# Small set-up work of a four-layer state-space kernel computed on VectorE in place of GpSimd, with a new order table

## The chip, the cores and the metric

The kernel runs on one core of a Trainium2 chip. The time is the device time of one execution in microseconds (us). Each kernel was run several times, and kernels that are compared ran on the same chip in the same rounds. All runs told here fell into one state: no run was more than 1.5% above the fastest of its kernel. The engines go by the names of the profile: PE is TensorE, PEld its weight loads, DVE is VectorE, ACT is ScalarE, POOL is GpSimd.

## The reference, cut to what matters

Two kinds of layers alternate, on a sequence of 2048 tokens with 640 channels: a complex diagonal state-space layer (S5) and a long convolution with a gate.

```python
x = x + A(layernorm(x))      # S5: 640 complex states
x = x + B(layernorm(x))      # gate times a long convolution of k*v
x = x + A(layernorm(x))      # the same weights again
x = x + B(layernorm(x))

def A(x):
    dt = exp(log_dt); Lam_bar = exp(dt * Lam)             # 640 complex numbers
    B_bar = ((Lam_bar - 1) / Lam)[:, None] * Bmat         # the S5 factor
    h[t] = Lam_bar * h[t-1] + x[t] @ B_bar.T
    return 2 * real(h @ Cmat.T) + x * Dskip

def B(q):
    k_shift = 4-tap causal convolution of k; kv = k_shift * v
    y = irfft(rfft(kv) * rfft(ssm_k)) + kv * ssm_D        # the same for both layers
    return q * y
```

`y` and the S5 weights depend on no layer's input. The kernel computes them in a set-up of some 165 us and then streams the layers' matmuls.

## The kernel before

A small planner in the kernel's own Python lists every piece of work as a task with an engine (or a choice of two), an estimated cost and what it depends on. It simulates the engines with these costs, takes the free task with the highest rank, and emits the tasks in the order of their simulated starts. The program fixes that order for each engine: a piece that is late holds up what stands behind it in its engine's queue (in the trace of after, an eviction starts at 31.23 us, behind 25 small instructions that take 3.3 us).

```python
t.rank = t.path + t.bias if WHEN is None else 0.001 * t.path - WHEN.get(t.name.partition(":")[0], 0)
...                                                       # cut
order.sort(key=lambda t: (t.start, t.idx))
for t in order:
    t.emit(t.eng)
```

`WHEN` is the order table: one number for a group of tasks ("a_b10" stands for all five tasks "a_b10:0" to "a_b10:4").

The two pieces of GpSimd work that the argument turns on multiply an identity by Lam_bar (15 diagonal matrices of 128 x 128, so that TensorE can scale B by matmuls), and compute the S5 factors in 24 instructions of five elements for each partition (a 25th, the reciprocal, is VectorE's):

```python
def diag(dst, scal, n):
    nc.gpsimd.tensor_tensor(dst, ident[:, None, :].to_broadcast([P, n, P]), scal[:, :, None].to_broadcast([P, n, P]), ALU.mult)

def e_lamd(_):                                            # L401 in the profile
    diag(s_ld.get().rearrange("p i j n -> p (i j) n"), st["lam"][:].rearrange("p i j -> p (i j)"), 15)
t_ld = S.add("a_lamd", "pool", 3.4, [t_lam], e_lamd, uses=[s_ld])

def e_f(_):                                               # L411 to L440
    v = nc.gpsimd
    v.tensor_tensor(den[:], lre, lre, ALU.mult)
    v.tensor_tensor(t2[:], lim, lim, ALU.mult)
    v.tensor_tensor(den[:], den[:], t2[:], ALU.add)
    nc.vector.reciprocal(inv[:], den[:])
    ...                                                   # 21 more of [128, 5], cut
t_f = S.add("a_f", "pool", 5.5, [t_lam], e_f)
```

Beside them stand, in the same stretch, the four-tap convolution of k (TensorE, L1064) with its eviction (a copy out of the matmuls' result memory, which is also the product with v), on VectorE (L1070), evictions of matmuls on ScalarE (L296) or VectorE (L298), and the first piece of a rotation table on VectorE (L552, L553).

## Time and profile before

| | before |
|---|---|
| time, median of 3 runs | 360.56 us (360.41 to 360.77) |
| span of the profiled run | 358.5 us |
| TensorE busy | 324.3 us, 90% |
| VectorE busy | 321.8 us, 90% |
| ScalarE busy | 253.2 us, 71% |
| GpSimd busy | 24.4 us, all of it before 60 us |

Two engines at 90% for the whole span leave little idle time on either for more work. They do not say which of them is the limit at a given time; for that one reads stretches of 10 us, which the prediction shows. One line also belongs here. It is the last 5 us in which TensorE still works (stretch; busy us of PE, PEld, DVE, ACT, POOL with instruction counts; PE clock, DMA share, GB/s):

```profile
345.00:350.00 5.00, 2.83 (x24) 1.64 (x23) 4.90 (x13) 1.99 (x6) 0.00 (x0) 1.00 0.30 121
```

TensorE is busy for 2.83 us after 345 us. The last matmuls in its timeline (start, duration, what) say the same:

```profile
347.10 0.72 PE L773 MATMUL ps<-W,b 128*128 128x128 bf16 x10
347.66 0.22 PE L773 MATMUL ps<-DD,b 128*128 128x128 bf16 x1
```

TensorE ends at 347.88 us and VectorE at 355.3 us.

### The profile page before, as it was taken

To read this page: it belongs to the slowest core of one execution; us is meant where nothing else is said; L and a number is where in the kernel's file an instruction comes from. 1 tells how busy PE (TensorE), PEld (TensorE's weight loads), DVE (VectorE), ACT (ScalarE), POOL (GpSimd) and SP (SyncE) were. 2 spreads that over 40 slices of the span, in tenths; PEclk is the share of its full clock that TensorE was granted. 3 is DMA by queue.
4 is the path that set the end of the run, shared out by engine and by line. 5 is a ranking of instruction groups with operands and counts; after the bars stand their busy time and mean duration, and the time that the engine had idled before them with its cause. 6 is when DMAs were issued, how large, how long until landed. Compare 5 with 4: busy or idle time off the path is not lost.

```text
span 358.5 us, 8291 instructions
## 1 busy us (share of the span) xinstructions
PE 324.3 (90%) x3467; PEld 242.3 (68%) x3493; DVE 321.8 (90%) x482; ACT 253.2 (71%) x399; POOL 24.4 (7%) x57
## 2 busy tenths in 40 slices
PE   2888899978997989999999999999999999999980
PEld 1357867867685978886776686688655788756550
DVE  8979999777899669989997998999999799999996
ACT  6589976989499999784598199796618681106861
POOL 6447200000000000000000000000000000000000
PEclk9999999999999999999999999999999999999996
DMA  9999999989996970966095722450032043000231
GB/s 202 227 169 190 205 193 196 235 156 201 241 249 125 237 159 2 144 121 206 2 206 140 273 76 48 117 129 2 14 61 76 0 112 112 1 2 0 85 136 73
DMA packets 118711, 45.90 MB, mean 128 GB/s; under 512 B 111629, under 2 KB 112914, under 8 KB 118674
## 3 DMA queue, kind: packets, MB, share of 16 engines
q1 hardware_dynamic: 118528, 45.36, 59.1%
q8 instruction: 27, 0.44, 0.5%
q14 instruction: 10, 0.08, 0.1%
q10 hardware_dynamic: 146, 0.01, 0.0%
HBM read 17.38 MB, written 7.86 MB: 70 GB/s over the span
## 4 chain that ended last, share of the span: by engine, by line
PE 62%; ACT 14%; DVE 11%; DMA 5%; issue 4%; POOL 2%; SPq 1%; ACTq 0%; DVEq 0%; POOLq 0%
PE ps L773 31%; PE ps L687 9%; PE ps L684 9%; ACT b L296 8%; PE ps L522 4%; PE ps L1064 4%; DMA b<-b 2%; DVE b L298 2%; ACT b L466 1%; DMA b<-in_A_C_im_dram 1%; DMA b<-in_A_C_re_dram 1%; SPq L462 1%; PE ps L1214 1%; DVE b L1070 1%; PE ps L1215 1%
## 5 line engine op out<-in xcount | busy, mean ns | idle before, releaser
L296 ACT ACTIVATE b<-ps 128x1024 bf16<-128x1024 f32 (+3 forms) x121 | 105.9, 957 | 28.9 <-PE ps L687 22.2
L773 PEld LDWEIGHTS <-b 128*128 128x128 bf16 x880 | 67.6, 98 | 48.2
L773 PE MATMUL ps<-W,b 128*128 128x512 bf16 (+1 forms) x632 | 95.4, 299 | 0.4
L684 PE MATMUL ps<-b,BT 128*128 128x256 bf16 x400 | 56.7, 273 | 2.4 <-ACT b L296 1.7
L687 PE MATMUL ps<-b,BT 128*128 128x256 bf16 x400 | 56.8, 273 | 0.0
L722 DVE TENSOR_TENSOR_SCAN b<-rtab,b 128x1290 bf16<-128x1290 f32 x16 | 44.6, 2832 | 0.2
L684 PEld LDWEIGHTS <-BT 128*128 128x128 bf16 x400 | 38.7, 98 | 7.2 <-issue 1.8
L687 PEld LDWEIGHTS <-BT 128*128 128x128 bf16 x400 | 39.1, 98 | 4.5
L595 ACT ACTIVATE junk<-b,nmean 128x640 bf16<-128x640 f32 x48 | 39.8, 828 | 1.5
L640 ACT ACTIVATE b<-b,nmr,rstd 128x640 bf16<-128x640 f32 (+1 forms) x42 | 35.7, 916 | 2.8 <-DVE nmr L607 2.0
L1133 PE MATMUL ps<-b,b 128*128 128x128 bf16 x170 | 35.1, 219 | 2.4 <-ACT b L296 1.4
L1136 PE MATMUL ps<-b,b 128*128 128x128 bf16 x170 | 35.3, 219 | 0.0
L1135 PE MATMUL ps<-b,b 128*128 128x128 bf16 x150 | 32.9, 220 | 0.0
L1138 PE MATMUL ps<-b,b 128*128 128x128 bf16 x150 | 32.9, 219 | 0.0
L298 DVE CAST b<-ps 128x1024 bf16<-128x1024 f32 (+2 forms) x28 | 28.0, 1024 | 4.7 <-PE ps L1138 2.3
L781 ACT ACTIVATE b<-ps 128x640 f32<-128x640 f32 x15 | 10.5, 701 | 26.4 <-PE ps L773 26.4
L773 PE MATMUL ps<-G,b 128*128 128x128 bf16 (+1 forms) x151 | 26.5, 295 | 0.5
L1064 PE MATMUL ps<-b,fd 128*128 128x512 bf16 x75 | 20.6, 415 | 2.8 <-ACT b L296 1.9
L470 DVE SCALAR_TENSOR_TENSOR W<-b,s_F 128x640 bf16<-128x640 bf16 x20 | 17.2, 880 | 3.7 <-ACT b L466 3.5
L466 ACT ACTIVATE b<-b,s_F 128x640 f32<-128x640 bf16 x20 | 16.5, 832 | 5.2 <-DMA b<-in_A_C_im_dram 4.0
L590 ACT ACTIVATE nmean<-sums 128x4 f32<-128x4 f32 (+1 forms) x15 | 3.0, 201 | 22.7 <-DVE b L785 19.3
L1214 PE MATMUL ps<-b,b 128*128 128x128 bf16 x160 | 18.4, 220 | 0.5 <-ACT b L296 0.5
(210 smaller groups left out, 571.6 us busy)
## 6 DMA issues: line engine op xcount, KB each, us to landing
b<-in_A_x_dram SPq DMA_DIRECT2D x8, 640.0 KB, 5.9
b<-ysd SPq DMA_DIRECT2D x8, 640.0 KB, 3.9
b<-in_B_ssm_k_dram SPq DMA_DIRECT2D x5, 512.0 KB, 6.4
kvd<-b SPq DMA_DIRECT2D x5, 512.0 KB, 3.8
b<-kvd SPq DMA_DIRECT2D x5, 512.0 KB, 5.1
ysd<-b SPq DMA_DIRECT2D x5, 512.0 KB, 4.6
out_dram<-b SPq DMA_DIRECT2D x8, 320.0 KB, 2.2
W<-in_A_B_im_dram SPq DMA_DIRECT2D x1, 800.0 KB
```

What stands on the lines that cost most here:

```text
L296: nc.scalar.activation(out, in_, ACT.Copy)
L298: nc.vector.tensor_copy(out, in_)
L595: nc.scalar.activation(small.junk, src(q), ACT.Square, bias=st["nmean"][:, i:i + 1], scale=1.0, accum_out=st["ssq"][:, i:i + 1])
L640: nc.scalar.activation(dst, src, ACT.Identity, bias=st["nmr"][:, i:i + 1], scale=st["rstd"][:, i:i + 1])
L684: nc.tensor.matmul(pb[:, jj, c2, :], lhsT=aw["BT1"][:, c2, j, k, :], rhs=uT[:, k, 0:2, :].rearrange("p t i -> p (t i)"), start=(k == 0), s ...
L687: nc.tensor.matmul(pb[:, jj, c2, :], lhsT=aw["BT0"][:, c2, k, j * P:(j + 1) * P], rhs=uT[:, k, 2:4, :].rearrange("p t i -> p (t i)"), star ...
L722: nc.vector.tensor_tensor_scan(gv, rt, gv, 0.0, ALU.mult, ALU.add)
L773: nc.tensor.matmul(pc[:, o0:o1], lhsT=lh, rhs=rh, start=(n == 0), stop=(n == len(ops) - 1))
L1064: nc.tensor.matmul(pk[:, 512 * b:512 * (b + 1)], lhsT=s_ds.get()[:, l, :], rhs=kT[:, t0:t0 + 512], start=(l == 0), stop=(l == 3))
L1133: nc.tensor.matmul(ps[:, g, 0, :], lhsT=T["Cf"].get()[:, q, :], rhs=are, start=True, stop=single)
L1135: nc.tensor.matmul(ps[:, g, 0, :], lhsT=T["Sf"].get()[:, q, :], rhs=A[:, 2 * q + 1, :], start=False, stop=True)
L1136: nc.tensor.matmul(ps[:, g, 1, :], lhsT=T["NSf"].get()[:, q, :], rhs=are, start=True, stop=single)
```

## The change

The intent: take the diagonal matrices of Lam_bar and the S5 factors off GpSimd, where they take 3.39 and 6.8 us and where an instruction of VectorE beside them (L552) takes 1.99 us, against 0.82 in after; cut the rest of GpSimd's work into shorter instructions; write LayerNorm rows contiguously and make one product of four; and give every task its own entry in the order table, with TensorE's slow start in the planner's simulation (it doubles TensorE's estimates before 16 us; in the trace of before, matmuls of 512 columns start 0.427 us apart until 17.6 us and 0.216 us apart after it). An entry of two numbers also says how much longer the task's first engine must be busy before its second may take it.

```diff
 WHEN = {
-    "yt_io0": -1077.9, "yt_ph0": -1019.3, "yt_sin0": 190.5, ...        # cut: one entry per group
+    "kv_mm0:0": 17.79, "kv_ev0:0": 19.87, ... "a_b1e0:0": (32.68, 1.5), ...   # cut: one per task
-            t.rank = t.path + t.bias if WHEN is None else 0.001 * t.path - WHEN.get(t.name.partition(":")[0], 0)
+            t.rank, t.wait = t.path + t.bias, 0.3
+            if WHEN is not None:
+                when = WHEN[t.name]
+                t.rank, t.wait = (-when[0], when[1]) if isinstance(when, tuple) else (-when, 0.3)
+                if eng == "pe" and now < self.COLD:                     # COLD = 16.0
+                    t.est *= 2.0
 # S5 set-up
-        diag(s_ld.get()..., st["lam"]..., 15)
-    t_ld = S.add("a_lamd", "pool", 3.4, [t_lam], e_lamd, uses=[s_ld])
+        diag(nc.vector, s_ld.get()..., st["lam"]..., 15)
+    t_ld = S.add("a_lamd", "dve", c_tt(15 * P), [t_lam], e_lamd, uses=[s_ld])    # 1.12
-        v = nc.gpsimd
-    t_f = S.add("a_f", "pool", 5.5, [t_lam], e_f)
+    t_f = S.add("a_f", "dve", 1.9, [t_lam], e_f)
-        diag(aw["DD"][:], st["pf"][:, 3, :], NJ)
+        for j in range(NJ):
+            diag(nc.gpsimd, aw["DD"][:, j:j + 1], st["pf"][:, 3, j:j + 1], 1)
 # four-tap convolution: the diagonals one at a time
-            nc.gpsimd.tensor_tensor(s_ds.get(), ident..., skf..., ALU.mult)      # [P, 4, P]
+            for l in range(4):
+                nc.gpsimd.tensor_tensor(s_ds.get()[:, l], ident, skf..., ALU.mult)   # [P, P]
 # LayerNorm rows contiguous
-                ln_apply(nc, eng, st, q, s_u.get()[:, :, slot, :], src(q).rearrange("p (k e) -> p k e", e=P))
+                ln_apply(nc, eng, st, q, s_u.get()[:, slot * D:(slot + 1) * D], src(q))
 # gate: one product for four rows
-                    nc.vector.tensor_tensor(b, b, s_Y.get()[:, q, :], ALU.mult)   # for each of 4 rows
+                    nc.vector.tensor_tensor(b, b, s_Y.get(), ALU.mult)            # once, 4 rows
```

Some of the planner's costs were changed too, by up to some 0.3 us. `c_tt(n)` is 0.1 + 0.00053 n, the planner's cost in us of a product of bf16 with bf16.

## The prediction

> **What bounds the kernel now.** I read the page first (busy shares and the slices), then stretches of 10 us, then the chain of waits, and last the timeline of the two places where the chain leaves TensorE: the set-up at 24 to 40 us and the end.
>
> ```profile
> span 358.5 us, 8291 instructions
> PE 324.3 (90%) x3467; PEld 242.3 (68%) x3493; DVE 321.8 (90%) x482; ACT 253.2 (71%) x399; POOL 24.4 (7%) x57
> PE   2888899978997989999999999999999999999980
> ```
>
> Two engines are at 90%, TensorE and VectorE, so neither can be relieved alone. The slices show TensorE short of full only in the first 18 (up to some 160 us) and in the last two. By stretches (busy us of PE, PEld, DVE, ACT, POOL):
>
> ```profile
> 20.00:30.00 10.00, 9.08 (x108) 6.78 (x109) 7.92 (x21) 9.92 (x21) 4.33 (x5) 1.00 0.95 161
> 30.00:40.00 10.00, 8.07 (x154) 6.84 (x152) 9.51 (x11) 9.44 (x15) 7.92 (x27) 1.00 1.21 228
> ...
> 300.00:310.00 10.00, 9.95 (x90) 8.68 (x89) 9.86 (x12) 2.42 (x3) 0.00 (x0) 1.00 0.01 3
> ...
> 340.00:350.00 10.00, 7.83 (x69) 4.85 (x68) 9.53 (x23) 6.36 (x16) 0.00 (x0) 1.00 0.39 136
> 350.00:360.00 10.00, 0.00 (x0) 0.00 (x0) 5.26 (x9) 0.85 (x3) 0.00 (x0) 0.60 0.17 66
> ```
>
> From 165 to 342 us TensorE streams without a break, and VectorE is nearly full beside it while ScalarE has room (2.42 of 10). After 342 us TensorE has no more matmuls, and VectorE works off a queue. The end of the chain of waits says the same (start, duration, what):
>
> ```profile
> 28.33 3.40 POOL b L401
> ...
> 338.08 3.82 PE ps L773 x28
> 341.92 0.83 DVE b L785 x2
> 343.20 0.82 DVE b L822
> ...
> 353.61 0.81 DVE b L805
> 354.44 0.89 DVE b L809
> ```
>
> The span has therefore three parts: some 165 us of set-up and long convolution where TensorE, VectorE and ScalarE take turns as the bound; 177 us of pure TensorE; and an end of 358.5 - 341.9 = 16.6 us, of which VectorE's queue is 355.3 - 341.9 = 13.4 and the last store 3.2. The one long GpSimd piece on the chain is the diagonal matrices of lambda, at 28.33. Its neighbourhood in the timeline:
>
> ```profile
> 28.33 3.39 POOL L401 TENSOR_TENSOR b<-ident_bf,s_lam 128x1920 bf16<-128x1920 bf16 x1 [1.74 <-DVE s_lam L395]
> 32.70 1.33 POOL L413 TENSOR_TENSOR s_den<-s_den,s_t 128x5 f32<-128x5 f32 x1
> ```
>
> ```profile
> 30.42 1.99 DVE L552 TENSOR_SCALAR b<-rtab 128x1290 f32<-128x1290 f32 x1
> 32.44 1.53 DVE L553 SCALAR_TENSOR_TENSOR b<-b,rtab 128x1290 f32<-128x1290 f32 x1
> ```
>
> L552 ends at 32.41, only 0.69 us after GpSimd let go at 31.72; L413, five elements wide, takes 1.33 us and ends at 34.03, just after L553 at 33.97. Each engine held the other up.
>
> [...] about 30.42 to 31.72, 1.3 us, of L552 is a wait. [...] L818 (all bf16, 640 wide) has a mean of 487 ns, L822 (one operand fp32, the same width) 825 ns. [...] the first 16 matmuls 512 wide in the chain take 5.91 us (369 ns each), a later run of 8 takes 1.73 us (216 ns). [...] 640 wide costs 487 ns, 2560 wide (L708) 1494, not 4 x 487 = 1948.
>
> **The change, part by part.**
>
> Lambda diagonals to VectorE. Removed from GpSimd: 3.39 us. Added to VectorE: 1920 elements. The scalars are fp32, so by the L822 rate (or L1070: 1024 in 1.22 us, 1.19 ns an element at most; slope between 640 at 825 and 1024 at 1220 is 1.03 ns) I expect 0.1 + 1.04 x 1920 = 2.1 us, not the 1.1 that the kernel's own table assumes. It takes away the 1.3 us wait of L552, and the matmuls on lambda can start 3.4 - 2.1 = 1.3 us earlier.
>
> S5 factors to VectorE. 24 small instructions that took GpSimd from 31.68 to 38.45, 6.8 us. On VectorE dependent small instructions start 0.21 us apart (24.11, 24.32, 24.52, 24.73 in the angle reduction), independent ones 0.07 to 0.15. With half of each: 12 x 0.21 + 12 x 0.1 = 3.7 us of VectorE. The first scaling of C (L466) started at 37.05, 0.34 us after its factor was ready at 36.71, so this was a real wait; now the factors may be ready 4 us earlier.
>
> Shorter GpSimd instructions (shift diagonals and skip diagonals one matrix at a time): the total stays near 5 x 1.05 + 1.25 = 6.5 us, but no VectorE instruction waits for a whole 1.05 us. At 12.93 one 128x1 instruction of VectorE (L963) took 1.04 us in place of 0.15; I count 1 us saved.
>
> LayerNorm rows written contiguously. The VectorE form with fp32 in is 745 ns over 12 uses; the one use near the end that already writes contiguously took 0.61. At most 12 x 0.15 + 6 x 0.1 = 2.4 us, say 1.5 since ScalarE does the larger part of them.
>
> One product for four rows: 28 x L818 at a start-to-start of 0.45 us (12.6) become 7 of 2560 at 1.45 (10.2): 2.4 us less VectorE, spread over the TensorE-bound part.
>
> VectorE in sum: + 2.1 + 3.7 - 1.3 - 1.0 - 1.5 - 2.4 = -0.4 us. Nothing, in total; but the additions lie before 40 us and the savings after 165, where VectorE's queue sets what is left for the end.
>
> TensorE: the same matmuls, so the same time. With N / 2.4 GHz + 2.8 ns for each (the 256-wide ones start 0.109 us apart) they come to 315 us; the stretch from the first matmul (6.4) to the last (341.9) is 335.5. About 20 us are gaps and cold clock (2.4 us of it in the 16 matmuls above), all before 165 us. Counting the cold clock changes no instruction: it only makes the order fit better there.
>
> The order table. Its entries grow like planned starts; I take no time from them, only the order. It puts all of the last layer's products but one row's ahead of the last matmuls: behind TensorE's end then lie one eviction with residual (0.75), four u and four m (8 x 0.80), two pairs of small statistics (0.7), and perhaps one row of the block before (0.8): 8.7 us, against 13.4. The end would be 4.7 us shorter. But this work is done earlier, in a stretch where VectorE already has 95% or more, so part of it comes back as a later end of TensorE unless evictions go to ScalarE. I give back 2.5 of it. In the first part the shorter wait for lambda and the factors are worth 1.3 on the chain, but VectorE was at 9.5 of 10 there and gets 5.8 us more work, less the 2.3 of waits: I count 0.5 us gained from the better packing. Sum: 4.7 - 2.5 + 0.5 = 2.7, so 360.56 - 2.7 = 357.8 us.
>
> **Rivals.** (a) The fine order closes the early gaps: of the 20 us some 6 could go, and with the shorter end the time would be about 351. For it: one entry for each task frees the four rows and the five groups from one common rank. Against it: in 20 to 60 us VectorE, ScalarE and TensorE all have over 80%, so a gap closed on one is opened on another, and the added VectorE work lies just there. (b) The mis-sized VectorE work (2.1 for 1.1, 3.7 for 1.9 assumed) pushes the whole fixed order back by the 2.8 us that the plan lacks, at a time when VectorE is the bound, and TensorE waits: 360 to 362. For it: queues are in order, so a late piece holds up all behind it. Against it: VectorE had 2 us idle in 20 to 30. (c) [...] its removal gives the full 4 us at which the factors come earlier: about 355. Against it: the table still loads C for the weights later than the factors are ready, so weights are not waiting for them.
>
> **Range and chances.** The middle is 357.8; (a) and (c) pull down, (b) up. 8 times in 10 between 353.5 and 361.2. Faster by over 2% means below 353.35, which needs (a) in the main: 0.11. Slower by over 2% means above 367.8, which nothing here but a badly held-up queue would do: 0.02. Within 2%: 0.87.
>
> **What would show it.** TensorE's busy time unchanged within 2 us, 177 us or a little more of unbroken TensorE at the end, VectorE's busy time within 3 us of 321.8, GpSimd down from 24.4 to about 15, the time from the last matmul to the last VectorE instruction 8 to 10 us in place of 13.4, and the lambda diagonals at about 2.1 us on VectorE. It is wrong if TensorE's last matmul ends before 338 us (early gaps closed), if the end stays at 13 us, or if a wait of TensorE on VectorE of over 2 us shows up in 25 to 45 us.

## The result and the profile after

| | before | after |
|---|---|---|
| time, median of 4 runs | 360.49 us (360.18 to 360.77) | 365.30 us (363.55 to 366.90) |
| ratio after/before | | 1.0133, 95% interval 1.0085 to 1.0180 |
| span of the profiled run | 358.5 | 365.2 |
| TensorE's last matmul ends | 347.88 | 353.95 |
| VectorE's last instruction ends | 355.3 | 361.98 |

A ratio is the mean time of one kernel's fast runs over that of the other's fast runs of the same rounds, so it is not quite the ratio of the medians beside it. The change made the kernel slower by 1.3%, about 4.8 us, outside the range on record. The profiled run of after is the slowest of its four (366.9), so of the 6.7 us between the spans some 1.6 belong to that run.

The page of after: span, busy times, PE's slices and the clock that it was granted (tenths of full speed, 40 slices of 9.1 us).

```profile
span 365.2 us, 8269 instructions
PE 327.1 (90%) x3463; PEld 246.1 (67%) x3493; DVE 319.6 (88%) x488; ACT 251.6 (69%) x397; POOL 22.9 (6%) x51
PE   2597998799987999999999999999999999999970
PEclk9998999999999899999999999999999999999995
```

VectorE has 2.2 us less work than before and TensorE 2.8 us more, for the same matmuls. The two slices of the clock that read 8 can account for these 2.8 us: the granted clock was halved for 3.41 us from 32.6 us and for 3.41 us from 118 us, in which the same matmuls take up to 3.4 us longer in all (those of 128 columns start 0.107 us apart instead of 0.056). The stretches (columns as above):

```profile
20.00:30.00 10.00, 9.03 (x97) 5.96 (x97) 9.59 (x26) 7.52 (x14) 3.69 (x11) 1.00 0.78 174
30.00:40.00 10.00, 7.60 (x115) 7.04 (x112) 7.45 (x20) 6.71 (x10) 0.00 (x0) 0.83 1.25 228
...
110.00:120.00 10.00, 7.43 (x96) 5.98 (x95) 9.76 (x28) 9.07 (x14) 0.00 (x0) 0.90 0.77 156
```

In 20 to 30 us VectorE went from 7.92 to 9.59: the moved work. In the next 10 us all three engines do less than before (TensorE 8.07 to 7.60, at a lower clock too; VectorE 9.51 to 7.45; ScalarE 9.44 to 6.71). When all engines are less busy at once, somebody waits for somebody. VectorE's queue from 24 us (start, duration, what):

```profile
24.76 2.16 DVE L487 TENSOR_TENSOR b<-ident_bf,s_lam 128x1920 bf16<-128x1920 bf16 x1
26.84 1.22 DVE L1169 TENSOR_TENSOR b<-ps,b 128x1024 bf16<-128x1024 f32 x1
27.97 0.30 DVE L496 TENSOR_TENSOR s_den<-s_pf 128x5 f32<-128x5 f32 x1
...
31.16 0.16 DVE L525 TENSOR_SCALAR s_F<-s_g 128x5 f32<-128x5 f32 x1
31.23 1.22 DVE L1169 TENSOR_TENSOR b<-ps,b 128x1024 bf16<-128x1024 f32 x1
32.37 0.82 DVE L638 TENSOR_SCALAR b<-rtab 128x1290 f32<-128x1290 f32 x1
```

The 25 small instructions of the factors (L496 to L525) hold the queue from 27.97 to 31.23, 3.3 us, and the eviction L1169 stands behind them. TensorE needs the buffer that this eviction empties:

```profile
30.06 0.22 PE L588 MATMUL ps<-b,tab 128*128 128x128 bf16 x1
32.51 0.22 PE L1232 MATMUL ps<-b,b 128*128 128x128 bf16 x1 [2.23 <-DVE b L1169]
...
33.03 0.31 PE L1235 MATMUL ps<-b,b 128*128 128x128 bf16 x1
33.14 0.31 PE L1237 MATMUL ps<-b,b 128*128 128x128 bf16 x1
```

The bracket is the reading: TensorE stood idle for 2.23 us and was released by that eviction. After it the matmuls of 128 columns start 0.107 us apart instead of 0.056, for 3.41 us: the granted clock was halved (0.50 in 34 to 36 us).

The end of the chain of waits, and TensorE's last group:

```profile
346.07 3.82 PE ps L859 x28
351.02 2.94 DVE b L924 x4
...
358.58 1.68 DVE b L905 x2
```

```profile
353.23 0.72 PE L859 MATMUL ps<-W,b 128*128 128x128 bf16 x10
```

The chain hands over from TensorE to VectorE at 349.9 us, while TensorE goes on until 353.95. From the last matmul to the last VectorE instruction are 8.0 us here and 355.3 - 347.9 = 7.4 us before. The end did not become shorter. So nearly all of the difference in the spans, 6.1 of 6.7 us, is that TensorE finishes later.

To see when TensorE falls behind, the matmuls that had been done by a given time were added up from the traces, each at its length at full clock by the planner's own cost (n / 2400 + 0.0028 us for n columns, as in the prediction, so 0.056, 0.109 and 0.216 us for 128, 256 and 512 columns, the distances at which such matmuls start in the trace of before; 316.1 us in all for each kernel). This table was worked out so; it is the lead (+) or lag (-) against before, in us of matmul work. Some matmul records are missing from the traces (3467 matmuls for 3493 weight loads before); second counts that treat the gaps otherwise agree with it within about 1.1 us, so only its larger steps should be read.

| by (us) | after | after, work on GpSimd | before, work on VectorE | before, factors alone on VectorE |
|---|---|---|---|---|
| 20 | -0.75 | -1.07 | +0.75 | +0.54 |
| 30 | -0.81 | -0.62 | +0.38 | +0.32 |
| 35 | -2.51 | +0.64 | -0.86 | +0.46 |
| 40 | -2.43 | +1.32 | -1.98 | -1.23 |
| 50 | -1.69 | +1.80 | -2.28 | -1.71 |
| 60 | -3.03 | -0.71 | -2.20 | -1.56 |
| 120 | -5.64 | -2.47 | -2.44 | -2.39 |
| 150 | -6.99 | -2.30 | -2.09 | -2.03 |
| 200 to 340 | -6.1 | -1.4 | -3.1 | -2.5 |

The last three columns are experiments, told next. After about 170 us no column changes any more: the rest is TensorE alone, and whatever is lost before is carried to the end.

### The profile page after: what moved, and what is told of

The parts are those of the page before. It is cut to its first block, busy times and chain, and to the rows that moved or that the text cites. A ratio compares the mean times of both kernels' runs of the same rounds, so it can differ in the third digit from the quotient of the medians.

```text
span 365.2 us, 8269 instructions
## 1 busy us (share of the span) xinstructions
PE 327.1 (90%) x3463; PEld 246.1 (67%) x3493; DVE 319.6 (88%) x488; ACT 251.6 (69%) x397; POOL 22.9 (6%) x51
## 4 chain that ended last, share of the span: by engine, by line
PE 65%; DVE 14%; ACT 8%; DMA 6%; issue 3%; SPq 2%; POOL 0%; DVEq 0%; ACTq 0%; POOLq 0%
PE ps L859 31%; PE ps L770 10%; PE ps L773 10%; ACT b L382 4%; PE ps L1163 2%; PE ps L1208 2%; DMA b<-in_B_v_dram 2%; DMA b<-kvd 2%; DVE bs L706 2%; DMA b<-in_A_x_dram 2%; DVE b L1169 2%; PE ps L1232 1%; PE ps L1235 1%; DMA b<-in_A_C_im_dram 1%; PE ps L1237 1%
## 5 line engine op out<-in xcount | busy, mean ns | idle before, releaser
L382 ACT ACTIVATE b<-ps 128x1024 bf16<-128x1024 f32 (+3 forms) x123 | 109.7, 949 | 33.4 <-PE ps L773 23.9
L859 PE MATMUL ps<-W,b 128*128 128x128 bf16 (+1 forms) x629 | 95.6, 298 | 0.6
L1232 PE MATMUL ps<-b,b 128*128 128x128 bf16 x170 | 35.9, 224 | 5.2 <-DVE b L1169 2.2
L726 ACT ACTIVATE b<-b,nmr,rstd 128x640 bf16<-128x640 f32 (+1 forms) x36 | 30.9, 912 | 8.6 <-DVE nmr L693 7.7
L1235 PE MATMUL ps<-b,b 128*128 128x128 bf16 x170 | 36.4, 225 | 0.0
L1237 PE MATMUL ps<-b,b 128*128 128x128 bf16 x150 | 33.9, 226 | 0.0
L1234 PE MATMUL ps<-b,b 128*128 128x128 bf16 x150 | 33.8, 225 | 0.0
L384 DVE CAST b<-ps 128x1024 bf16<-128x1024 f32 (+2 forms) x26 | 26.4, 1024 | 7.6 <-issue 3.4
L1313 PE MATMUL ps<-b,b 128*128 128x128 bf16 x160 | 19.6, 219 | 3.1 <-ACT b L382 2.5
L1314 PE MATMUL ps<-b,b 128*128 128x128 bf16 x160 | 19.5, 219 | 1.1 <-DVE b L1294 1.1
L1163 PE MATMUL ps<-b,fd 128*128 128x512 bf16 x74 | 19.1, 394 | 1.2 <-DVE b L1169 0.7
L552 ACT ACTIVATE b<-b,s_F 128x640 f32<-128x640 bf16 x20 | 16.8, 841 | 3.2 <-DMA b<-in_A_C_im_dram 2.0
```

The costliest lines, as they stand in the source:

```text
L382: nc.scalar.activation(out, in_, ACT.Copy)
L726: nc.scalar.activation(dst, src, ACT.Identity, bias=st["nmr"][:, i:i + 1], scale=st["rstd"][:, i:i + 1])
L859: nc.tensor.matmul(pc[:, o0:o1], lhsT=lh, rhs=rh, start=(n == 0), stop=(n == len(ops) - 1))
L1163: nc.tensor.matmul(pk[:, 512 * b:512 * (b + 1)], lhsT=s_ds.get()[:, l, :], rhs=kT[:, t0:t0 + 512], start=(l == 0), stop=(l == 3))
L1232: nc.tensor.matmul(ps[:, g, 0, :], lhsT=T["Cf"].get()[:, q, :], rhs=are, start=True, stop=single)
L1234: nc.tensor.matmul(ps[:, g, 0, :], lhsT=T["Sf"].get()[:, q, :], rhs=A[:, 2 * q + 1, :], start=False, stop=True)
```

## The experiments

The theory after reading the two traces was that of the queue (Q): the moved work stands in VectorE's queue between 25 and 40 us, in front of evictions that TensorE needs, and the delay is carried to the end. The rivals: the new order table itself is worse; the half clock that follows a gap of TensorE is what costs; the planner was given wrong costs, and right ones would have led to a good order; and, for the hope behind the change, that it gains something if VectorE no longer waits beside GpSimd's long instructions. Fifteen kernels were run; all gave correct results. The time after "against" is that of the kernel before in the same rounds. It lay between 359.64 and 360.50 us, so the ratio is to be read, rather than the absolute times of the expectations. After itself was timed in four runs only: its 1.0133 is known to about 0.5%, so a difference from after of less than 0.5% (1.7 us) is not clear of the noise.

### First: the move and the order apart

**after, with both pieces of work on GpSimd.** The order is planned as in after; only the engine that computes is put back.

```diff
-        diag(nc.vector, s_ld.get()..., 15)
+        diag(nc.gpsimd, s_ld.get()..., 15)
     def e_f(_):
+        v = nc.gpsimd
```

> The changed kernel with the lambda diagonals and the S5 factors emitted on GpSimd again; the order of every engine's other work stays as in the changed kernel. Theory Q (queue: the 2.16 and 3.3 us now stand in VectorE's queue ahead of a PSUM product that TensorE waits for, the gap at 30 to 32.5 us, and the half clock that follows it): the gap and the half clock at 32.6 to 36 us go, some 4 us, so 361 to 362 us. Rival O (order: the new table itself is worse, whatever engine does these two): 364 to 366, as the changed kernel. Rival G (GpSimd takes 3.4 and 6.8 us for them, TensorE waits for the diagonals): a wait on GpSimd of over 1 us before the lambda matmuls, 363 or more.

Measured: 361.87 us (361.80 to 362.21, 5 runs) against 359.82; ratio 1.0061 [1.0045, 1.0078]. Putting the work back on GpSimd gives back 1.0133 / 1.0061 = 1.0072, 0.7% or 2.6 us (give or take 0.5%). The remaining 0.6% (2.2 us) is there with all the arithmetic on its old engine. Rival G fell: the list of TensorE's waits in 24 to 48 us is empty here.

**before, with both on VectorE.** Again the order stays as it was planned.

```diff
-        diag(s_ld.get()..., 15)
+        nc.vector.tensor_tensor(s_ld.get()..., ident..., st["lam"]..., ALU.mult)
     def e_f(_):
-        v = nc.gpsimd
```

> The kernel before with only these two pieces of work moved to VectorE, order table and all else as before. Theory Q: VectorE is full from 26 to 50 us, so 5.5 us more of work[...] delays its evictions: 362 to 364 us. Rival O: the move itself is harmless, 359.5 to 361.

Measured: 363.57 us (362.66 to 364.81, 5 runs) against 359.82; 1.0108 [1.0082, 1.0134]. In the order for which it was not planned the move costs 1.1%. TensorE's timeline shows two gaps with VectorE's eviction as the releaser (in the brackets):

```profile
31.68 0.22 PE L502 MATMUL ps<-b,W 128*128 128x128 bf16 x1 [2.09 <-DVE b L298]
...
38.21 0.40 PE L1110 MATMUL ps<-FA,b 64*128 64x128 bf16 x8 [1.18 <-DVE b L298]
```

The move is a loss in the old order and in the new one.

**after, with the factors behind the next eviction.** In VectorE's queue the 25 instructions trade places with the eviction that they held up.

```diff
         order.sort(key=lambda t: (t.start, t.idx))
+        move task "a_f" to just behind task "kv_ev1:0"
```

> The changed kernel with one task moved: the S5 factors (24 small VectorE instructions) go behind the next PSUM product of the shift convolution rather than ahead of it. Theory Q: TensorE's gap at 30 to 32.5 us closes and no half clock follows, the time falls by 3 to 4 us to 361 to 362.5. Rival O: the time stays at 364 to 366, because what is won at 35 us is lost again in the waits at 100 to 150 us.

Measured: 363.60 us (362.83 to 363.97, 4 runs) against 359.82; 1.0103 [1.0083, 1.0124]. The gap of 2.23 us and the half clock at 32.6 us are gone (the mean granted clock of the run is 0.979 all the same, as in after); the longest wait of TensorE on VectorE in 24 to 48 us is now this one (waits: us in total, times, longest):

```profile
PE ps L591 <- DVE BT L388: 1.1, 1, 1.1
```

TensorE's lag at 40 us is gone (within the 1.1 us of the count), but at 60 us it lags by 1.0 and at the end by 2.8. Only 0.3% came back, less than the noise of after. So that one gap does not explain the loss: in this trace it was closed and nearly all of the loss stayed. That the 3.3 us of VectorE then make another eviction late (the 1.1 us above) is a reading of the trace.

**after, with the true costs given to the planner.**

```diff
-    t_ld = S.add("a_lamd", "dve", c_tt(15 * P), ...)
+    t_ld = S.add("a_lamd", "dve", 2.1, ...)
-    t_f = S.add("a_f", "dve", 1.9, ...)
+    t_f = S.add("a_f", "dve", 3.3, ...)
```

> The changed kernel with the two assumed costs in its planner set to what the trace shows (2.1 us for the diagonals in place of 1.12, 3.3 for the factors in place of 1.9), the table the same; the planner then orders some tasks differently. Theory Q (in the form that the undersized costs made the fixed order wrong): 360 to 362.5 us. Rival O: 364 to 366.

Measured: 381.20 us (379.77 to 382.12, 5 runs) against 359.82; 1.0587 [1.0560, 1.0614]. The expectation was far off, and the rival that right costs would mend it fell. The order table is a list of ranks for one simulation; with two costs changed by 1 us and 1.4 us the simulation can take other tasks at its free moments, and the resulting order was worse by some 16 us than that of after. Where these 16 us arise was not looked into. This table, at least, was not mended by correcting those costs.

### Second: which piece, and is it the clock?

**before, with the diagonals alone on VectorE:**

```diff
-        diag(s_ld.get()..., 15)
+        nc.vector.tensor_tensor(s_ld.get()..., ident..., st["lam"]..., ALU.mult)
```

> The kernel before, with the lambda diagonals alone on VectorE (the factors stay on GpSimd). Theory Q: the 2.15 us piece stands ahead of one PSUM copy at 28.3 us, TensorE then waits some 2 us for it and falls to half clock for 3.4 us: 361.5 to 363. Rival D (they cost only together, because VectorE runs out of slack): 359.5 to 360.5.

Measured: 360.89 us (360.29 to 361.51, 9 runs) against 359.66; 1.0033 [1.0020, 1.0047]. It is milder than the theory of the queue expected. Part of the reason is in the views: the rotation table's L552 took 1.99 us beside the GpSimd piece before, and 0.83 us in the run with both pieces on VectorE, so the move gives some 1.2 us back. And the wait that it makes for TensorE (second line) stands in place of a wait for GpSimd's diagonals before (first line), so that it adds 0.9 us and not 2:

```profile
PE ps L501 <- POOL b L401: 1.2, 1, 1.2
PE ps L501 <- DVE b L298: 2.1, 1, 2.1
```

**before, with the factors alone on VectorE:**

```diff
     def e_f(_):
-        v = nc.gpsimd
```

> The kernel before, with the S5 factors alone on VectorE (the lambda diagonals stay on GpSimd[...]). Theory Q: 3.3 us stand ahead of a PSUM copy near 35 us; TensorE has other work there, so a wait of about 1 us and no half clock: 360.5 to 362. Rival D: 359.5 to 360.5.

Measured: 363.51 us (361.18 to 364.15, 5 runs) against 359.66; 1.0093 [1.0064, 1.0122]. The 25 instructions of five elements cost more than the 1920-element product. Both together (0.33% + 0.93%) come to the 1.08% of both at once, within the intervals. TensorE's longest wait in 24 to 48 us:

```profile
PE ps L1108 <- DVE b L298: 2.7, 1, 2.7
```

The delay is carried on: a group of 16 matmuls of the long convolution just after it (L1109 of before) starts at 39.55 us instead of 37.52 (+2.0), the last matmul of the kernel at 350.16 instead of 347.66 (+2.5).

**after, with TensorE kept busy over the gap.** One group of ten matmuls on Lam_bar is computed five times over, to fill the gap of 2.23 us with work that changes nothing.

```diff
-                for k in range(NJ):
+                for k in (5 if (c, j) == (1, 0) else 1) * list(range(NJ)):
```

> The changed kernel with one group of ten matmuls on lambda computed five times over in place of once (the same values, 2.2 us of idle TensorE filled), just ahead of its wait for VectorE's late PSUM product at 30 us. Theory C (the half clock at 32.6 to 36 us is set off by the idle stretch, and costs what it takes from TensorE, at most 1.7 us): no half clock there, 363.5 to 364.5 against 365.3. Rival N (the half clock is not what costs; TensorE is behind VectorE there anyway): 365 to 366, or more, since one eviction comes 2.2 us later.

Measured: 364.56 us (363.47 to 364.69, 5 runs) against 359.66; 1.0126 [1.0109, 1.0142]. The half clock at 32.6 us is gone from the trace (one of 3.41 us appears at 71.4; the mean granted clock of the run is 0.986, of after 0.979), and the time is that of after within the intervals. But the most that theory C allowed, 1.7 us, is no more than the uncertainty of after, so this run can't rule it out. A second look at the same question needs no new kernel: among 111 runs of the kernel before, the 51 with a mean granted clock under 0.988 have a median of 359.86 us, the 60 others 360.15 (in two of the four sets of rounds they were the faster ones, in two the slower). So in the kernel before, a lower clock did not go with a longer time. In the kernels with the moved work this stays open: the five runs with the factors alone on VectorE took 361.18 us at a mean clock of 0.992, 362.74 at 0.985, and 363.51 to 364.15 at 0.975 to 0.979. Whether the clock makes part of the time there, or longer gaps make both, was not tested. But the loss does not need it: in the profiled run of that kernel the clock was full from 16 to 118 us (1.00 in the stretches of 20 to 50 us, 0.92 in 110 to 120), and its TensorE was 2.0 us late at 40 us already and 2.5 at the end.

**after on GpSimd, with its diagonals whole again.** This is the first experiment with the skip and shift diagonals in one instruction each, as before.

```diff
-            for l in range(4):
-                nc.gpsimd.tensor_tensor(s_ds.get()[:, l], ident, skf..., ALU.mult)
+            nc.gpsimd.tensor_tensor(s_ds.get(), ident..., skf..., ALU.mult)
```

> The changed kernel with everything of GpSimd's as before (diagonals and factors on GpSimd, shift and skip diagonals in one instruction each); the new table, the contiguous rows and the merged product stay. If splitting the GpSimd instructions hurts (one group of four took 5.65 us beside VectorE's products): 360.5 to 361.3. If it is harmless and the new order itself costs the rest: 361.5 to 362.3, as with the two pieces moved back alone.

Measured: 362.93 us (362.50 to 363.31, 5 runs) against 359.66; 1.0088 [1.0072, 1.0105]. Against the first experiment, cutting GpSimd's instructions is worth 1.0088 / 1.0061, 0.27% or 1 us, in the new order. The two runs come from different rounds and the difference is known to about 0.2%, so that this part of the change helps is likely, but only just clear of the noise.

### Third: parts of the change that might have been worth keeping

**before, with contiguous LayerNorm rows.**

```diff
-                ln_apply(nc, eng, st, q, s_u.get()[:, :, slot, :], src(q).rearrange("p (k e) -> p k e", e=P))
+                ln_apply(nc, eng, st, q, s_u.get()[:, slot * D:(slot + 1) * D], src(q))
                                                           # and the views of what reads these rows, cut
```

> The kernel before with one part of the change alone: LayerNorm rows written contiguously, so that VectorE's form takes some 0.6 us in place of 0.745. It saves VectorE at most 2.4 us. If VectorE's queue carries the end, 358.5 to 360; if it hides behind TensorE, 360 to 360.7.

Measured: 359.79 us (358.54 to 361.01, 22 runs) against 359.64; 1.0000 [0.9987, 1.0012]. The instructions did become faster. In the kernel before (count, busy us, mean ns of one):

```profile
L642 DVE TENSOR_SCALAR b<-b,rstd,nmr 128x640 bf16<-128x640 f32 x12 | 8.7, 745 | 0.4
L642 DVE TENSOR_SCALAR b<-b,rstd,nmr 128x640 bf16<-128x640 bf16 x6 | 3.3, 597 | 0.0
```

and with contiguous rows:

```profile
L642 DVE TENSOR_SCALAR b<-b,rstd,nmr 128x640 bf16<-128x640 f32 x12 | 7.1, 610 | 0.4
L642 DVE TENSOR_SCALAR b<-b,rstd,nmr 128x640 bf16<-128x640 bf16 x6 | 2.4, 439 | 0.0
```

VectorE saves (8.7 - 7.1) + (3.3 - 2.4) = 2.5 us, and the kernel saves nothing.

**before, with GpSimd's diagonals of Lam_bar in five pieces,** so that no instruction of VectorE has a GpSimd instruction of 3.39 us beside it:

```diff
-        diag(s_ld.get()..., 15)
+        for j in range(NJ):
+            nc.gpsimd.tensor_tensor(s_ld.get()[:, :, j, :], ident..., st["lam"][:, :, j:j + 1]..., ALU.mult)
```

> The kernel before with the lambda diagonals left on GpSimd but in five instructions, one for each block of 128 states. [...] VectorE no longer waits 1.3 us for the whole of it, and TensorE starts its lambda matmuls 2.5 us earlier (its wait of 1.25 us goes): 358.5 to 359.8. Rival: nothing changes at the end, since TensorE is not the bound there: 360 to 360.7.

Measured: 360.18 us (358.55 to 361.46, 22 runs) against 359.64; 1.0011 [1.0000, 1.0022]. No gain. GpSimd's timeline, then VectorE's (L553 and L554 are L552 and L553 of before):

```profile
27.38 5.83 POOL L405 TENSOR_TENSOR b<-ident_bf,s_lam 128x384 bf16<-128x384 bf16 x5 [1.73 <-DVE s_lam L395]
```

```profile
29.48 1.00 DVE L553 TENSOR_SCALAR b<-rtab 128x1290 f32<-128x1290 f32 x1
30.51 2.01 DVE L554 SCALAR_TENSOR_TENSOR b<-b,rtab 128x1290 f32<-128x1290 f32 x1
```

L553 takes about 1 us less than before (1.99 to 1.00), but L554 takes 0.5 more (1.53 to 2.01), and the five pieces take 5.83 us where the whole took 3.39.

**before, with both of these.** The edit is the last two diffs in one kernel:

```diff
+                ln_apply(nc, eng, st, q, s_u.get()[:, slot * D:(slot + 1) * D], src(q))
+        for j in range(NJ):
+            nc.gpsimd.tensor_tensor(s_ld.get()[:, :, j, :], ident..., st["lam"][:, :, j:j + 1]..., ALU.mult)
```

> Both of the last two together in the kernel before. If the gains add: 357.5 to 359.5. If neither reaches the end: 360 to 360.7.

Measured: 360.35 us (359.30 to 361.27, 13 runs) against 359.64; 1.0018 [1.0005, 1.0030]. No gain either; if anything it is slower, by 0.2%.

### Fourth: dose, and relief

If VectorE in 25 to 40 us is the limit, more work there must cost more, and less must gain.

**before, factors on VectorE, computed twice:**

```diff
     def e_f(_):
-        v = nc.gpsimd
-    t_f = S.add("a_f", "pool", 5.5, [t_lam], e_f)
+    t_f = S.add("a_f", "pool", 5.5, [t_lam], lambda _: (e_f(0), e_f(0)))
```

> The kernel before with the S5 factors on VectorE and computed twice over (the second time writes the same values), so 6.6 us in place of 3.3. Queue theory, carried to the end: another 2.5 to 3.3 us over the run with them once (3.3 us or 0.93% over before), so 365.5 to 367. Accident: less than 1 us more, 362.5 to 364.5.

Measured: 369.12 us (366.99 to 369.56, 5 runs) against 360.50; 1.0231 [1.0199, 1.0263]. Once costs 0.93%, twice 2.31%: the second 3.1 us of VectorE add 1.38%, about 5 us (give or take 1.5). TensorE's wait on the same eviction goes from 2.7 to 5.8 us, by just the length of the second copy:

```profile
PE ps L1108 <- DVE b L298: 5.8, 1, 5.8
```

That the total grows by more than 3.1 was not expected. In this trace TensorE's clock is low in 40 to 50 us as well (0.68), and its lag, counted as in the table, is between 3 and 5 us at 40 and between 5 and 6 at 50; whether the low clock is the cause there was not tested.

**after, with the factors alone on GpSimd:**

```diff
     def e_f(_):
+        v = nc.gpsimd
```

> The changed kernel with the factors alone back on GpSimd, the diagonals on VectorE. If the factors are the cost in the new order too: 361.5 to 362.8, as with both moved back (1.0061 of before). If it is the diagonals: 364 to 366.

Measured: 363.23 us (362.33 to 363.48, 5 runs) against 360.50; 1.0070 [1.0043, 1.0097]. That is as good as having both on GpSimd (1.0061), so in the new order too it is the factors that cost most of what the move costs, as far as the noise of after lets one tell.

**before, with the rotation table's first piece moved** from 30 us to 63 us, in VectorE's queue, which takes 3.5 us off VectorE just where it is full:

```diff
         order.sort(key=lambda t: (t.start, t.idx))
+        move task "a_t0" to just behind task "kv_ev3:1"
```

> The kernel before with the two VectorE instructions of the rotation table (3.5 us at 30 us[...]) moved to a gap of VectorE at 63 us; nothing needs them before 115 us. Queue theory: the stretch at 28 to 40 us gets 3.5 us back and TensorE is ahead by 1 to 3 us from there to the end: 357 to 359 against 359.7. Accident, or another engine next to bound: 359.3 to 360.2.

Measured: 360.32 us (358.98 to 361.43, 22 runs) against 360.50; 0.9993 [0.9980, 1.0006]. No gain. The stretch of 30 to 40 us of this kernel (PE, PEld, DVE, ACT, POOL):

```profile
30.00:40.00 10.00, 8.08 (x154) 6.83 (x152) 6.18 (x9) 9.45 (x14) 6.41 (x27) 1.00 1.21 226
```

VectorE fell from 9.51 to 6.18. TensorE (8.07 to 8.08) and ScalarE (9.44 to 9.45) did not move. ScalarE is nearly full in this stretch too, which would explain why relief of VectorE alone lets nobody go faster. ScalarE was not relieved in any run, so this cause is argued and not shown; that the relief gains nothing is measured.

**before, both pieces on VectorE, and the rotation table later:**

```diff
-        diag(s_ld.get()..., 15)
+        nc.vector.tensor_tensor(s_ld.get()..., ident..., st["lam"]..., ALU.mult)
     def e_f(_):
-        v = nc.gpsimd
+        move task "a_t0" to just behind task "kv_ev3:1"
```

> The same move of the rotation table, with diagonals and factors on VectorE as in the change, order otherwise as before. Queue theory: 2.3 us of VectorE work leave the crowded stretch, so of the 1.08% (3.9 us) that the move to VectorE costs some 2.3 come back: 360.5 to 361.8. If it then also profits from the earlier diagonals, below 360. Accident: 363 to 364, as without the move.

Measured: 361.83 us (360.55 to 362.90, 18 runs) against 360.50; 1.0036 [1.0024, 1.0049]. Here the same step gives back 0.72% of the 1.08% that the move costs. The step is worth nothing where VectorE has just enough time, and two thirds of the loss where it has too little. This is the strongest support for the queue, since the same relief is tested with and without the added work.

### What the experiments say together

VectorE's time between 25 and 40 us was just used up in the kernel before. Work added there delays evictions, TensorE waits for them, and nothing later takes the delay up: from 170 us on TensorE streams without a break (before, it is busy for 174.19 of the 175 us from 165 to 340). Work taken away there gained nothing (0.9993). The price is one-sided.

Of the 1.33%, about 0.7 (between 0.2 and 1.2) is the move of the two pieces to VectorE, most of it the factors; the old order, with closer timing, gives 1.08 for the same move. The other 0.6% comes with the rest of the new version. Its cut GpSimd pieces probably help (0.27%) and its contiguous rows did nothing in the old order, which leaves 0.9% for its order table with the product of four rows, as the run with whole diagonals shows (1.0088). That order was planned with both pieces on VectorE, at 1.12 and 1.9 us, so 0.9% is what it costs with them on GpSimd; no order planned for that was tried. Where TensorE loses it can be seen. In the first experiment, after on GpSimd, TensorE is ahead of before by 1.8 us at 50 us, and behind by 0.7 at 60 and 2.5 at 120. The stretch in which its busy time falls furthest behind, before and then in that experiment (PE, PEld, DVE, ACT, POOL):

```profile
50.00:60.00 10.00, 9.67 (x126) 7.04 (x125) 9.92 (x11) 6.89 (x10) 1.16 (x2) 1.00 1.12 221
50.00:60.00 10.00, 7.88 (x112) 6.02 (x113) 9.93 (x10) 9.25 (x13) 1.12 (x1) 1.00 0.91 191
```

TensorE has 7.88 where it had 9.67. Its waits there are 1.5 us for evictions on ScalarE, which has 9.25 where it had 6.89, and 0.6 for VectorE, which is full in both. In 110 to 120 us it loses again (8.23 to 7.07), with ScalarE full (10.00): its waits in 108 to 122 us are 2.8 us for ScalarE's evictions and 0.2 for VectorE's. Which entries of the table cause this, and whether the product of four, which needs all four rows at once, has a part in it, was not separated and stays open. No version was clear of the noise faster than the kernel before: the best, with the rotation table later, has a ratio of 0.9993, the same.

## Why the prediction was wrong

It said 357.8 us, 353.5 to 361.2; the time is 365.3. In the order of its own steps:

| step | predicted | measured |
|---|---|---|
| diagonals on VectorE | + 2.1 us of VectorE | 2.16 |
| factors on VectorE | + 3.7 | 3.3 (27.97 to 31.23) |
| wait of L552 gone | - 1.3 | - 1.2 (1.99 to 0.82) |
| LayerNorm rows | - 1.5 | - 2.5 (in the old order) |
| one product for four rows | - 2.4 | - 3.2 (13.6 to 10.4) |
| VectorE in all | - 0.4 | - 2.2 (321.8 to 319.6) |
| the end after TensorE | - 4.7 | + 0.6 (7.4 to 8.0) |
| of it given back to TensorE | + 2.5 | does not apply |
| first part | - 0.5 | TensorE ends 6.1 later in the profiled runs |

**The costs of single operations were right, or nearly.** The diagonals, the lifted wait, and which instructions are left after the last matmul (one eviction, four u, four m and two pairs of small ones) came out as worked out; the factors (3.3 for 3.7), the rows and the product of four came out somewhat cheaper for VectorE.

**The first step that failed is "After 342 us TensorE has no more matmuls".** The chain of waits left TensorE at 341.9 us, and the prediction took this for TensorE's end. A chain leaves an engine when the last thing needed comes from another engine; that does not mean that the first has stopped. The lines shown in the prediction already spoke against it: with an end at 341.9, TensorE could have been busy for 1.9 us at most in 340 to 350, and the line says 7.83. So the end before was not 13.4 us but 7.4, the 8.7 predicted for after (measured: 8.0) was no gain, and the 4.7 us, which was the whole reason for a faster kernel, did not exist. The same early end went into "About 20 us are gaps and cold clock": 335.5 us is 6 us short, and the 315 us of matmuls are some 5.6 short, since 26 matmul records of 512 columns are missing from that trace (those with all 3493 come to 321.6). The two errors cancel, so the 20 us are right by luck. With this term and the 2.5 given back struck out, the same sum gives 360.56 - 0.5 = 360.1: still too low, but "the same" instead of a gain.

**The second is "I count 0.5 us gained from the better packing"**, the term of the sum for the first part. Its sign was wrong. The prediction saw that VectorE had 9.5 of 10 busy and got 5.8 us more work less 2.3 of waits, and it named the outcome as rival (b), 360 to 362. Then it let the 3.5 us be absorbed by the packing. The move cost 0.7% (2.6 us) in the new order and 1.1% (3.8 us) in the old one, so the net addition of 3.5 us was paid about one to one. Nor did "in 20 to 60 us VectorE, ScalarE and TensorE all have over 80%", on which rival (a) was turned down, read the lines rightly: its own line for 20 to 30 us has VectorE at 7.92 of 10, and ScalarE has 6.89 in 50 to 60. The argument against rival (b), "VectorE had 2 us idle in 20 to 30", did not hold: in after that idle time was used (9.59), and TensorE waited still. The idle time could not be filled with this work: in the kernel before, 1.91 us of it ended at 23.63 us, where VectorE waited for ScalarE's exp of the time step, and Lam_bar, on which the diagonals and the factors hang, is computed from that.

**The third is "Nothing, in total", the sum of -0.4 us for VectorE.** The sum of an engine over the whole span says nothing if the additions lie where it is the limit and the savings where it is not. VectorE saved 2.2 us in total, and the kernel became slower. That savings after 165 us are worth nothing unless they shorten the end was hinted at ("the additions lie before 40 us and the savings after 165"), but not put into the number. The experiment with contiguous rows shows it alone: 2.5 us of VectorE, ratio 1.0000.

**The new order table was not sized.** The prediction took only the order from it and gave rival (a) a gain of up to 6 us. It was a loss of 0.9% (with the product of four rows, and with the two pieces on GpSimd). None of the views of the kernel before that were read could tell it; an unsized term belongs on both sides of the range, and the prediction put it on the fast side alone.

**GpSimd at about 15 us was wrong:** it has 22.9. The 20 single shift diagonals take 12.0 us, 629 ns each in the mean, where five whole ones took 5.2. GpSimd was not the limit then, and the pieces probably still helped a little (0.27%), but for the number it was a miss.

**Rivals.** (b) is what happened, in that added VectorE work made TensorE wait, and with more than its size, since the loss by the order came on top. Its reason, that the planner's costs were too low, was not shown: right costs made 381.20 us, and in the old order, which was not planned for the move at all, the move cost as much. (c), the wait of L552 beside GpSimd's piece as the hidden cost, fell: the wait went away as predicted (1.99 to 0.82 us) and gained nothing, and the two experiments on GpSimd pieces in the old order gained nothing. Of the marks that the prediction set itself, "a wait of TensorE on VectorE of over 2 us in 25 to 45 us" came true, with 2.23 us, at 30.28 us. TensorE's busy time moved by 2.8 us and not under 2; two stretches of half clock can account for it.

VectorE took less time for the same products than GpSimd: 2.16 against 3.39 us for the diagonals (1.6 times), 3.3 against 6.8 us for the factors (2.1 times). The kernel's time does not follow these durations: GpSimd, with 24.4 us of work in all, had room for this, and VectorE had not. Of the prediction's own readings of single operations, that of TensorE's clock is loose: 369 against 216 ns is 1.7 times and not 2, since the granted clock became full at 17.57 us, while those 16 matmuls (12.96 to 18.87 us) were running. Apart, they show the factor of two, 0.427 us from start to start until 17.6 us and 0.216 after it, as does the spacing of 0.107 against 0.056 us in after.

## What to carry to other kernels

Before work is moved to a faster engine, look at the stretch where it will stand, not at the sum: VectorE was full there, and here each us was paid about in full and carried to the end, while the slower engine with room did it at next to no cost. To learn when an engine ends, read the engine's own last instruction; the chain of waits can leave an engine before it has finished, as here at 341.9 us against 347.88. And a saving on an engine counts only if no other one is at its limit in the same stretch: try the relief alone (as with the rotation table) before trusting it.

## What the traces measured beside this

- Beside a busy VectorE (27.2 to 32.5 us in the run with five pieces, 28.2 to 34.0 in before), the pieces cost GpSimd far more than the whole: 5.83 us against 3.39 us. Of the five groups of four single shift diagonals in after (1.05 us each as one instruction in before), four took 1.46 to 1.83 us, and the one at 50 us, where VectorE was busy for 9.90 of 10 us, took 5.65. VectorE's longer time went over to its next instruction (L552 of before 1.99 to 1.00 us, L553 1.53 to 2.01).
- After a gap of 2.23 us in after, TensorE's granted clock was halved for 3.41 us; after one of 2.09 us (both pieces on VectorE) the matmuls of 128 columns started 0.107 us apart as well. Gaps of 2.7 us (factors alone) and 2.1 us (diagonals alone) were not followed by it: the granted clock was 1.00 in 20 to 50 us of both. What sets the half clock off was not shown.
- In the chain of the factors, small instructions that depend on each other started 0.20 us apart, independent ones 0.07; the 25 took 3.3 us.
- 3.3 us of small instructions ahead of one eviction cost 0.93% of the whole kernel (3.3 us of 360), and twice as many 2.31%.
